# Moving two more tiles' inverse into the first down projection, and running the row halves of gate and up in two staggered passes

## The chip, the cores and the metric

The kernel runs on one core of one Trainium2 chip. The metric is the device time of one execution in microseconds (us), taken as the median of several executions. The span of the profile is about 2.0 us shorter than the time of the same execution.

## The reference, cut to what matters

```python
S, D, F = 2048, 576, 4608
h  = x + irfft2(rfft2(layernorm(x)) * (w_r + 1j * w_i))     # spectral mixing
n  = layernorm(h)
h2 = h + (gelu(n @ w_gate) * (n @ w_up)) @ w_down           # gated feed-forward
```

Everything is bf16 with f32 accumulation. The 2048 rows are 16 tiles of 128. The feed-forward takes them in four blocks of four tiles (512 columns of the moving operand).

## The kernel before: the parts that matter

TensorE makes the matmuls and leaves their sums in banks of PSUM; VectorE, ScalarE and POOL do the element-wise work. A helper records the operations of every engine in program order and derives the semaphore waits from named tiles (`r=` reads, `w=` writes). So each engine is handed its own list in this order, and a wait stands wherever an operand or a PSUM bank is not ready.

**Inverse transform.** For tile `c`, `st_I` makes 6 matmuls and a copy to SBUF; `st_N` makes 4 more, and VectorE adds the result to `x`. Ten tiles are done up front (`NPRE = 10`), the other six later.

**Way into the feed-forward.** The first four tiles are normalised by VectorE or POOL and transposed on TensorE (`turn_pe`, 5 small matmuls), and ScalarE copies the transpose to SBUF as `HT0`.

```python
TURN = (8, 9, 9, 9)                    # after which inverse tile each transpose stands
for c in range(1, NPRE):
    if c >= 2: st_I(c)
    st_N(c - 1)
    ...                                # squares, statistics
    if c == 6: ln2_b(0); ln2_c(0); norm(0, DVE); norm(1, POOL)
    if c == 7: norm(2, DVE); norm(3, POOL)
    for i in range(4):
        if TURN[i] == c: turn_pe(i)
```

**Gate and up.** D = 576 is 4.5 times 128, so the contraction is cut in slices of 64 rows: each output column needs 9 matmuls on the lower row half of the array and 9 on the upper half. In this kernel's trace a matmul of one half, which the program has write another bank, runs together with one of the other half: 648 of them take 70.05 us, a pair 0.216 us, while six without a partner take 1.45 us. Before, half 1 lags six positions behind half 0:

```python
ASEQ = [(0, i) for i in range(4)] + [(0, 8)] + [(1, 4 + i) for i in range(4)]   # half 0: gate, then up
BSEQ = [(0, i) for i in range(4)] + [(1, 4 + i) for i in range(4)] + [(1, 8)]   # half 1
LAG = 6
def gu(n):
    for s_ in range(9 * (n - 1) + LAG, 9 * n + LAG):
        for half in range(2):
            m, j = divmod(s_ - LAG * half, 9)
            ...
            b = 2 * (m % 3) + o                       # three pairs of PSUM banks
            P.op(PE, ... matmul(bank(b), ...[h0:h0 + 64, ...]))
    if n == 0:
        st_N(NPRE - 1)                                # last inverse tile, behind the first 6 matmuls
        return
    P.op(ACT, ... GL <- gelu(gate bank))
    P.op(DVE, ... AT[f] <- GL * up bank)              # the product
```

So the first six matmuls of half 0 have no partner: the last inverse tile, which needs the whole array, follows. In blocks 1 to 3 the columns are made in the order f = 9 ... 35, 0 ... 8.

**Down projection.** Each unit (half of a tile's columns) sums f = 0 ... 35. In block 0 each unit also carries the inverse of one deferred tile in a cheaper form (`def_i`, 8 small matmuls, then `def_n`, 2 matmuls).

```python
for h, (d0, d1) in enumerate(((0, cut), (cut, D))):
    b = (6, 7, 2, 3)[2 * (p % 2) * (tb > 0) + h]
    cd = NPRE + 2 * p + h if tb == 0 else NT
    if cd < NT: def_i(cd)
    for f in range(36):
        if cd < NT and f == 28: def_n(cd)
        P.op(PE, ... matmul(bank(b), AT[:, f, ...], WD[:, f, d0:d1], start=(f == 0), stop=(f == 35)))
    P.op(DVE, ... OS <- bank(b) + XO)                 # the output add
```

## Time and profile before

| what | value |
|---|---|
| time, median of 3 | 501.17 us (501.12 to 501.2) |
| the profiled execution | 502.36 us, span 500.6 us |
| TensorE busy | 490.3 us, 98% |
| a pair of half-row matmuls | 70.05 us / 324 = 0.216 us |
| a down matmul | 35.39 us / 288 = 0.123 us |

The page of the kernel before: busy time of TensorE, its granted clock in 40 slices of 12.5 us (9 is 90% or more), and the two costliest groups of matmuls.

```profile
PE 490.3 (98%) x4323; PEld 297.6 (59%) x4323; DVE 192.9 (39%) x418; ACT 159.3 (32%) x299; POOL 38.4 (8%) x51
...
PEclk9999989999999999999999999999999999999999
...
L920 PE MATMUL PS<-HT,WG 64*128 64x512 bf16 x2106 | 233.7, 378 | 0.9 <-ACT HT L862 0.9
...
L973 PE MATMUL PS<-WD,AT 128*128 128x288 bf16 (+2 forms) x1152 | 143.6, 286 | 0.0
```

The 378 ns of a group's mean are the time from start to end of one matmul, not its cost: the matmuls overlap in the trace, 324 pairs in 70.05 us. So the pace has to be read from the chain. The last columns say that TensorE waited 0.9 us in all before the gate/up matmuls and not at all before the down matmuls.

The chain of waits of the kernel before, in order of time: start, duration, what.

```profile
66.16 1.96 ACT HT L862 x3
...
68.26 1.45 PE PS L920 x6
69.71 0.86 PE PS L813 x4
70.57 71.42 PE PS L920 x648
...
172.10 9.80 PE PS L973 x80
181.90 70.05 PE PS L920 x648
251.94 35.39 PE PS L973 x288
287.33 70.05 PE PS L920 x648
```

The dense stream starts at 70.57 us. Block 0 takes 71.42 us where the others take 70.05: its first part ran at half clock. I call such a stretch of half clock a cut. The same profile by microsecond (TensorE busy, then granted clock, DMA share, GB/s):

```profile
69.00:70.00 1.00, 1.00 (x7) 0.95 1.00 300
70.00:71.00 1.00, 1.00 (x7) 0.50 1.07 373
71.00:72.00 1.00, 1.00 (x8) 0.50 1.01 378
72.00:73.00 1.00, 1.00 (x6) 0.50 1.05 396
73.00:74.00 1.00, 1.00 (x10) 0.84 0.97 369
```

The end of gate/up and the start of down in block 1 (timeline: start, duration, engine):

```profile
250.96 0.60 ACT L932 ACTIVATE GL<-PS 128x512 bf16<-128x512 f32 x1 [1.35 <-PE PS L920]
...
251.88 4.34 PE L973 MATMUL PS<-WD,AT 128*128 128x288 bf16 x34
252.05 0.69 DVE L933 TENSOR_TENSOR AT<-GL,PS 128x512 bf16<-128x512 bf16 x1 [1.26 <-PE PS L920]
```

The GELU of the last column is over at 251.56 us, before down starts. Its product ends at 252.74 us. The ninth step of down, which needs it, is due at 251.94 + 8 x 0.123 = 252.92 us. So it just fits, by 0.18 us.

### The profile page before, as it was taken

The page shows a single profiled execution, that of the slowest core. Times are in us where ns is not written, and L with a number is a line of the kernel's source. Part 1 is how long each engine was busy: PE and PEld are TensorE (multiplying, and loading weights), DVE is VectorE, ACT ScalarE, POOL GpSimd, SP SyncE. Part 2 cuts the span into 40 slices and gives each one's busy share as a digit, 9 for nine tenths or more (in the row PEclk, how much of TensorE's full clock was granted, in tenths as well). Part 3 has the DMA queues.
Part 4 walks back from the last instruction along what each step waited for, and adds up shares of the span by engine and source line. Part 5 has one row for each costly group of instructions (what it writes and reads, how often), then busy time and mean ns, then how long its engine had stood idle before and what let it go on. Part 6 is the DMA issues. An engine that isn't in the chain of part 4 may idle for free.

```text
span 500.6 us, 10028 instructions
## 1 busy us (share of the span) xinstructions
PE 490.3 (98%) x4323; PEld 297.6 (59%) x4323; DVE 192.9 (39%) x418; ACT 159.3 (32%) x299; POOL 38.4 (8%) x51
## 2 busy tenths in 40 slices
PE   6899989999999999999999999999999999999998
PEld 2688744444468864444477744444677544444775
DVE  6899643344355424433311134433200233333111
ACT  7888755342321322323300033232100123233000
POOL 3553270100000000000000000000000000000000
PEclk9999989999999999999999999999999999999999
DMA  8765796601000061100000001100000000000000
GB/s 277 171 199 197 254 356 243 214 14 25 18 7 14 19 211 32 22 14 1 2 13 12 19 18 22 22 1 1 1 18 19 13 1 2 1 2 1 12 19 19
DMA packets 27164, 31.40 MB, mean 63 GB/s; under 512 B 11664, under 2 KB 20112, under 8 KB 27120
## 3 DMA queue, kind: packets, MB, share of 16 engines
q1 hardware_dynamic: 24224, 18.81, 13.1%
q0 software_dynamic: 2896, 11.95, 6.7%
q8 instruction: 34, 0.56, 0.5%
q14 instruction: 10, 0.08, 0.1%
HBM read 26.42 MB, written 2.36 MB: 57 GB/s over the span
## 4 chain that ended last, share of the span: by engine, by line
PE 90%; DVE 6%; issue 1%; ACT 1%; DMA 1%; DVEq 0%
PE PS L920 57%; PE PS L973 28%; DVE TP L667 2%; PE PS L774 2%; DVE ST L468 1%; PE PS L813 1%; DVE ZS L672 1%; PE PS L628 1%; PE PS L940 1%; DVE CUS L641 1%; PE PS L691 1%; DMA XO<-in_A_x_dram 1%; DVE U L533 0%; ACT HT L862 0%; PE PS L657 0%
## 5 line engine op out<-in xcount | busy, mean ns | idle before, releaser
L920 PE MATMUL PS<-HT,WG 64*128 64x512 bf16 x2106 | 233.7, 378 | 0.9 <-ACT HT L862 0.9
L920 PEld LDWEIGHTS PS<-HT,WG 64*128 64x128 bf16 x2106 | 113.1, 94 | 117.7 <-issue 3.8
L932 ACT ACTIVATE GL<-PS 128x512 bf16<-128x512 f32 x144 | 85.8, 597 | 256.9 <-PE PS L920 256.1
L933 DVE TENSOR_TENSOR AT<-GL,PS 128x512 bf16<-128x512 bf16 x144 | 99.0, 688 | 174.5 <-PE PS L920 171.0
L973 PE MATMUL PS<-WD,AT 128*128 128x288 bf16 (+2 forms) x1152 | 143.6, 286 | 0.0
L973 PEld LDWEIGHTS PS<-WD,AT 128*128 128x128 bf16 x1152 | 110.8, 98 | 30.9 <-issue 1.3
L920 PE MATMUL PS<-HT,WGX 64*128 64x512 bf16 x486 | 56.9, 376 | 0.0
L976 DVE TENSOR_TENSOR OS<-PS,XO 128x288 bf16<-128x288 f32 (+2 forms) x32 | 14.7, 458 | 103.6 <-PE PS L973 103.6
L920 PEld LDWEIGHTS PS<-HT,WGX 64*128 64x128 bf16 x486 | 27.0, 94 | 27.3 <-PE PS L920 0.3
L712 POOL TENSOR_SCALAR WS<-WS 128x290 bf16<-128x290 bf16 x16 | 16.4, 1027 | 9.1 <-DMA WS<-in_A_w_i_dram 8.0
L628 PE MATMUL PS<-FT,U 128*128 128x290 bf16 x96 | 14.4, 287 | 0.5 <-DVE U L533 0.5
L691 PE MATMUL PS<-VT,ZS 128*128 128x256 bf16 x102 | 13.5, 272 | 0.2 <-DVE ZS L672 0.2
L667 DVE TENSOR_TENSOR TP<-YS,WS 128x580 bf16<-128x580 bf16 (+2 forms) x32 | 13.4, 457 | 0.3 <-issue 0.3
L704 ACT ACTIVATE V<-PS 128x768 bf16<-128x768 f32 x15 | 12.0, 811 | 1.0 <-PE PS L691 0.9
L804 ACT ACTIVATE JD<-XO 128x576 bf16<-128x576 bf16 x6 | 4.1, 684 | 24.8 <-DVE XO L957 24.8
L660 ACT ACTIVATE YS<-PS 128x578 bf16<-128x578 f32 x16 | 10.5, 655 | 3.5 <-PE PS L657 2.7
L522 PE MATMUL PS<-ATS,XO 128*128 128x128 bf16 (+1 forms) x80 | 7.1, 223 | 4.1 <-POOL ATS L495 2.7
L657 PE MATMUL PS<-CUS,BT 128*128 128x289 bf16 (+2 forms) x96 | 10.7, 246 | 0.3 <-DVE CUS L641 0.3
L628 PEld LDWEIGHTS PS<-FT,U 128*128 128x128 bf16 x96 | 9.2, 98 | 3.0 <-issue 0.7
L691 PEld LDWEIGHTS PS<-VT,ZS 128*128 128x128 bf16 x102 | 9.3, 97 | 1.7 <-issue 0.6
L816 DVE SCALAR_TENSOR_TENSOR XO<-PS,XO 128x576 bf16<-128x576 f32 x10 | 7.5, 755 | 6.7 <-PE PS L813 6.7
L468 DVE BATCH_NORM_STATS2 ST<-XO 128x6 f32<-128x288 bf16 x22 | 8.4, 445 | 3.8 <-DMA XO<-in_A_x_dram 3.8
(74 smaller groups left out, 200.4 us busy)
## 6 DMA issues: line engine op xcount, KB each, us to landing
WD<-in_B_w_down_dram POOLq DMA_DIRECT2D x9, 576.0 KB, 10.3
WG<-in_B_w_up_dram SPq DMA_DIRECT2D x4, 1152.0 KB, 6.6
WG<-in_B_w_gate_dram POOLq DMA_DIRECT2D x4, 1152.0 KB, 9.9
out_dram<-OS SPq DMA_DIRECT2D x30, 72.0 KB, 1.6
XO<-in_A_x_dram SPq DMA_DIRECT2D x3, 576.0 KB, 7.8
WGX<-in_B_w_gate_dram POOLq DMA_DIRECT2D x1, 1152.0 KB, 6.0
WGX<-in_B_w_up_dram SPq DMA_DIRECT2D x1, 1152.0 KB, 5.9
HT<-HN SPq DMA_TRANSPOSE x60, 2.4
```

Source lines behind the costliest of these rows:

```text
L468: P.op(DVE, lambda v, c=c, h=h: v.bn_stats(ST1[:, c, h, :], XO[:, c, 288 * h:288 * h + 288]), r=[("X", c)], w=[("ST1", c, h)])
L628: P.op(PE, lambda t, b=b, o=o, dt=dt, us=us, g=g: t.matmul(bank(b, 0, 128, 0, 2 * HK), U[:, us, g, :, :], FT[:, o, dt, :], start=(dt == 0) ...
L657: P.op(PE, lambda t, b=b, tb=tb, pl=pl, q0=q0, q1=q1, m=m, s3=s3, sp_=sp_: t.matmul(bank(b, 0, 128, q0, q1), BT[:, sp_, tb, :], CUS[:, s3, ...
L667: P.op(DVE, lambda v: v.tensor_tensor(out, YS[:, sl, :, q0:q1], WS[:, g, w_, q0:q1], op=ALU.mult), r=[("Y", sl), ("Wn", i), "Yz", "Zz"] + ...
L691: P.op(PE, lambda t, b=b, o=o, zp=zp, lhs=lhs, sp_=sp_, m=m, n=len(parts): t.matmul(bank(b, 0, 128, o, o + 256), lhs, VT[:, sp_, zp, :], s ...
L704: P.op(ACT, lambda a, dst=dst, src=src: a.activation(dst, src, ACTF.Copy), r=[("PS", bs[0]), ("PS", bs[2])], w=[("V", g, c) for c in range ...
L712: P.op(POOL, lambda v, g=GORD[i]: v.tensor_scalar(WS[:, g, 0, :], WS[:, g, 2, :], -1.0, None, op0=ALU.mult), r=[k for k in wkeys[0 if 1 <= ...
L920: op = P.op(PE, lambda t, h0=h0, kt=kt, wt=wt, f=f, slot=slot, b=b, HT=HT, s=(half == 0 and j in (0, 5)), e=(half == 1 and j in (3, 8)): t ...
L932: P.op(ACT, lambda a, s2=s2, b0=b0: a.activation(GL[:, s2, :], bank(b0), ACTF.Gelu_apprx_tanh), r=[("PS", b0)], w=[("GL", s2)])
L933: P.op(DVE, lambda v, s2=s2, b0=b0, f=f: v.tensor_tensor(AT[:, f, :], GL[:, s2, :], bank(b0 + 1), op=ALU.mult), r=[("GL", s2), ("PS", b0 + ...
L973: P.op(PE, lambda t, b=b, d0=d0, d1=d1, f=f, p=p: t.matmul(bank(b, 0, 128, 0, d1 - d0), AT[:, f, 128 * p:128 * p + 128], WD[:, f, d0:d1], ...
L976: P.op(DVE, lambda v, b=b, d0=d0, d1=d1, p=p, c=c: v.tensor_tensor(OS[:, p % 2, d0:d1], bank(b, 0, 128, 0, d1 - d0), XO[:, c, d0:d1], op=A ...
```

## The change

The intent: eight tiles' inverse moves into the first down projection instead of six, and the inverse in front is reordered so that normalisation and transposes start earlier, in smaller batches (three tiles, then one). Gate and up get a new order: in a first pass half 0 works on gate and half 1 on up (5 matmuls each), in a second pass they swap (4 each), and the second pass of a column follows the first pass of the next. Each pair of matmuls is thus complete from the first one on. It takes four pairs of PSUM banks, so the down projection moves from banks 6 and 7 to 0 and 1.

```diff
-NPRE = 10
+NPRE = 8
...
-    QR = ((0, 4), (4, NPRE), (NPRE, NT))
+    QR = ((0, 3), (3, 4), (4, NPRE), (NPRE, NT))
...
+    st_N(4); sq(3); ln2_c(0)                  # (one call a line in the source)
+    norm(0, DVE); norm(1, POOL); norm(2, POOL)
+    ln2_a(1); st_I(6); ln2_b(1); st_N(5); st_I(7); ln2_c(1)
+    norm(3, DVE)
+    turn_pe(0, ACT); st_N(6); turn_pe(1, DVE); turn_pe(2, ACT); turn_pe(3, ACT)
+    st_N(7)
...
+    FIRST = ([(0, i) for i in range(4)] + [(0, 8)], [(1, 4 + i) for i in range(4)] + [(1, 8)])
+    SECOND = ([(1, 4 + i) for i in range(4)], [(0, i) for i in range(4)])
+    def gu_part(m, second):
+        seqs = SECOND if second else FIRST
+        for j in range(len(seqs[0])):
+            for half in range(2):
+                o, wt = seqs[half][j]
...
-                b = 2 * (m % 3) + o
+                b = 2 * (m % 4) + o
...
-            b = (6, 7, 2, 3)[2 * (p % 2) * (tb > 0) + h]
+            b = (0, 1, 2, 3)[2 * (p % 2) * (tb > 0) + h]
...
-                if cd < NT and f == 28:
+                if cd < NT and f == 22:
...
-            gu(36 * tb + f + 1)
+            gu_part(36 * tb + f, False)
+            if f:
+                gu_part(36 * tb + f - 1, True)
...
+        gu_part(36 * tb + 35, True)
```

More of the change, by code (lines that the diff above doesn't have):

```diff
@@ L760, in _build @@
     vkeys = vk[0] + vk[1] + vk[2]
-    TURN = (8, 9, 9, 9)
-    seq = [("I", 0), ("I", 1)]
-    for c in range(2, NPRE):
-        seq += [("I", c)] + [("T", i) for i in range(4) if TURN[i] == c]
-    seq = {k: i % 2 for i, k in enumerate(seq)}
+    ISEQ = [("I", c) for c in range(8)] + [("T", i) for i in range(4)]
+    seq = {k: i % 2 for i, k in enumerate(ISEQ)}
     def islot(c):
@@ L836, in ln2_c, with lq @@
         P.op(DVE, lambda v, c0=c0, c1=c1: v.reciprocal(RS2[:, c0:c1], RS2[:, c0:c1]), r=[("SD2", q)], w=[("RS2", q)])
+    def lq(c):
+        return sum(c >= q0 for q0, _ in QR) - 1
     def norm(c, eng=DVE):
         hs = c % 4
-        q = (c >= 4) + (c >= NPRE)
+        q = lq(c)
         for i, (o0, o1, x0, x1) in enumerate(((0, D, 0, D), (D, 640, 512, D))):
@@ L852, in turn_dma, with turn_pe @@
                   r=[("HN", hs, 0), ("HN", hs, 1)], w=[("HT", q % 2, c % 4, k)], transpose=True)
-    def turn_pe(c):
+    def turn_pe(c, eng):
         hs = c % 4
@@ L859, in turn_pe, with sq @@
             b, o = b0 + k // 4, 128 * (k % 4)
-            P.op(PE, lambda t, b=b, o=o, k=k, hs=hs: t.matmul(bank(b, 0, 128, o, o + 128), HN[:, hs, 128 * k:128 * k + 128], IDT[:, :], start=True, stop=True),
+            lhs = HN[:, hs, 128 * k:128 * k + 128]
+            P.op(PE, lambda t, b=b, o=o, lhs=lhs: t.matmul(bank(b, 0, 128, o, o + 128), lhs, IDT[:, :], start=True, stop=True),
                  r=[("HN", hs, 0), ("HN", hs, 1), "IDT"], w=[("PS", b)])
-        P.op(ACT, lambda a, t0=t0, t1=t1, b0=b0: a.activation(HT0[:, 0:5, t0:t1], PS[:, b0 * 512:b0 * 512 + 640].rearrange("p (k e) -> p k e", k=5), ACTF.Copy),
-             r=[("PS", b0), ("PS", b0 + 1)], w=[("HT", 0, c, 0)])
-    st_I01()
-    for c in range(1, NPRE):
-        if c >= 2:
-            st_I(c)
-        st_N(c - 1)
-        if 2 <= c < 6:
-            square(c - 2, OS[:, c % 2, :], ("OS", c % 2, 0))
-        if c == 5:
-            ln2_a(0)
-        if c == 6:
-            ln2_b(0)
-            ln2_c(0)
-            norm(0, DVE)
-            norm(1, POOL)
-        if c == 7:
-            norm(2, DVE)
-            norm(3, POOL)
-        for i in range(4):
-            if TURN[i] == c:
-                turn_pe(i)
+        dst, src = HT0[:, 0:5, t0:t1], PS[:, b0 * 512:b0 * 512 + 640].rearrange("p (k e) -> p k e", k=5)
+        fn = (lambda a: a.activation(dst, src, ACTF.Copy)) if eng == ACT else (lambda v: v.tensor_copy(dst, src))
+        P.op(eng, fn, r=[("PS", b0), ("PS", b0 + 1)], w=[("HT", 0, c, 0)])
+    def sq(c):
+        square(c, OS[:, c % 2, :], ("OS", c % 2, 0))
+    st_I01()
+    st_N(0)
+    st_I(2)
+    st_N(1)
+    sq(0)
+    st_I(3)
+    st_N(2)
+    sq(1)
+    st_I(4)
+    st_N(3)
+    sq(2)
+    ln2_a(0)
+    st_I(5)
+    ln2_b(0)
+    st_N(4)
+    sq(3)
+    ln2_c(0)
+    norm(0, DVE)
+    norm(1, POOL)
+    norm(2, POOL)
+    ln2_a(1)
+    st_I(6)
+    ln2_b(1)
+    st_N(5)
+    st_I(7)
+    ln2_c(1)
+    norm(3, DVE)
+    turn_pe(0, ACT)
+    st_N(6)
+    turn_pe(1, DVE)
+    turn_pe(2, ACT)
+    turn_pe(3, ACT)
+    st_N(7)
     P.alias(ukeys + [(n_, a) for n_ in ("CU", "SU") for a in range(3)], [("WD", j) for j in range(9)])
@@ L895, in _build @@
     fnew = ([("AT", f) for f in range(36)] + [("GL", 0), ("GL", 1)] + [("HT", 1, i, k) for i in range(4) for k in range(5)])
-    ASEQ = [(0, i) for i in range(4)] + [(0, 8)] + [(1, 4 + i) for i in range(4)]
-    BSEQ = [(0, i) for i in range(4)] + [(1, 4 + i) for i in range(4)] + [(1, 8)]
-    LAG = 6
-    half_done = {}
     def fidx(m):
         return m % 36 if m < 36 else (m % 36 + 9) % 36
-    def gu(n):
-        for s_ in range(9 * (n - 1) + LAG, 9 * n + LAG):
-            for half in range(2):
-                m, j = divmod(s_ - LAG * half, 9)
-                if not 0 <= m < 144:
-                    continue
-                tb, f = m // 36, fidx(m)
-                slot = f // 9 if m < 27 else (3, 1, 2, 0)[f // 9]
-                o, wt = (ASEQ, BSEQ)[half][j]
+    FIRST = ([(0, i) for i in range(4)] + [(0, 8)], [(1, 4 + i) for i in range(4)] + [(1, 8)])
+    SECOND = ([(1, 4 + i) for i in range(4)], [(0, i) for i in range(4)])
+    first_done = {}
+    def gu_part(m, second):
+        tb, f = m // 36, fidx(m)
+        slot = f // 9 if m < 27 else (3, 1, 2, 0)[f // 9]
+        HT = HTS[tb % 2]
+        seqs = SECOND if second else FIRST
+        n = len(seqs[0])
+        for j in range(n):
+            for half in range(2):
+                o, wt = seqs[half][j]
                 kt = 4 if wt == 8 else wt % 4
                 h0 = 64 * half
-                HT = HTS[tb % 2]
-                b = 2 * (m % 3) + o
-                aft = [half_done[m, o]] if half and (j == 0 or j == 4) else []
-                op = P.op(PE, lambda t, h0=h0, kt=kt, wt=wt, f=f, slot=slot, b=b, HT=HT, s=(half == 0 and j in (0, 5)), e=(half == 1 and j in (3, 8)): t.matmul(
+                b = 2 * (m % 4) + o
+                aft = [first_done[m, o]] if second and j == 0 else []
+                op = P.op(PE, lambda t, h0=h0, kt=kt, wt=wt, b=b, s=(not second and j == 0), e=(second and j == n - 1): t.matmul(
                     bank(b), wg_tile(slot)[h0:h0 + 64, wt, 128 * (f % 9):128 * (f % 9) + 128], HT[h0:h0 + 64, kt, :], start=s, stop=e),
@@ L923, in gu @@
                     w=[("PS", b)], after=aft)
-                if half == 0:
-                    half_done[m, o] = op
-        m = n - 1
-        if m < 0:
-            st_N(NPRE - 1)
-            P.alias(fdead, fnew)
+                if not second:
+                    first_done[m, o] = op
+        if not second:
             return
-        s2, b0, f = m % 2, 2 * (m % 3), fidx(m)
-        P.op(ACT, lambda a, s2=s2, b0=b0: a.activation(GL[:, s2, :], bank(b0), ACTF.Gelu_apprx_tanh), r=[("PS", b0)], w=[("GL", s2)])
-        P.op(DVE, lambda v, s2=s2, b0=b0, f=f: v.tensor_tensor(AT[:, f, :], GL[:, s2, :], bank(b0 + 1), op=ALU.mult),
+        s2, b0 = m % 2, 2 * (m % 4)
+        P.op(ACT, lambda a: a.activation(GL[:, s2, :], bank(b0), ACTF.Gelu_apprx_tanh), r=[("PS", b0)], w=[("GL", s2)])
+        P.op(DVE, lambda v: v.tensor_tensor(AT[:, f, :], GL[:, s2, :], bank(b0 + 1), op=ALU.mult),
              r=[("GL", s2), ("PS", b0 + 1)], w=[("AT", f)])
@@ L978, in down @@
             P.dma(SP, ov[:, c, d0:d1], OS[:, p % 2, d0:d1], f"so{p % 2}{h}", r=[("OS", p % 2, h)], w=[("OUT", p % 2, h)])
-    gu(0)
+    P.alias(fdead, fnew)
     for tb in range(4):
         for f in range(36):
-            gu(36 * tb + f + 1)
+            gu_part(36 * tb + f, False)
+            if f:
+                gu_part(36 * tb + f - 1, True)
             if tb == 0 and f == 10:
@@ L987, in _build @@
             if tb == 0 and f < NPRE - 4:
-                square(4 + f, OS[:, f % 2, :], ("OS", f % 2, 0))
-            if tb == 0 and f == 13:
-                ln2_a(1)
-                ln2_b(1)
-                ln2_c(1)
+                sq(4 + f)
+            if tb == 0 and f == 8:
+                ln2_a(2)
+                ln2_b(2)
+                ln2_c(2)
             f0, f1 = (15, 3) if tb == 0 else (2, 4)
@@ L999, in _build @@
         if tb == 0:
-            ln2_a(2)
-            ln2_b(2)
-            ln2_c(2)
+            ln2_a(3)
+            ln2_b(3)
+            ln2_c(3)
             P.alias(vkeys + ["DP", "ITD", "EB", "Q0", "Q1", "YB0", "YB1", "JD"], [("WG", 3, k) for k in range(4)])
```

## The prediction

> **What bounds the kernel now.** TensorE. The page has PE busy 490.3 of 500.6 us; the chain of waits gives it 90%, 57% in the gate/up matmuls and 28% in the down projection. In order of time, that chain gives gate/up of row blocks 1 to 3 70.05 us each (324 pairs of 64-row matmuls at 0.216 us) and down 35.39 us (288 matmuls at 0.123 us), without a gap. [...] Only the seams can change.
>
> **Seam 1, the inverse (53.1 to 70.6 us).** Each tile costs PE 0.75 + 0.49 us, so two tiles fewer remove 2.5 us. Six gate/up matmuls that run without a partner at 68.3 us (1.45 us; six others stand unpaired at the end of block 3, within its 70.05) go too. Against this, transposes now wait: POOL takes 1.5 us per normalised tile, so tile 2 is ready near 64.7 us; VectorE works off its list in order, so its copy of transpose 1 ends near 66.5 and holds transpose 3, which shares its banks. I estimate the full stream starts at 67.8 us, against 70.6: -2.8. Before, the granted clock fell to 0.5 from 70 to 73.2 us, and block 0 took 71.4 instead of 70.05. With more PE idle before it I expect about 1.7 us lost again in block 0: -2.4 in all at the end of gate/up 0.
>
> **Seam 2, first down.** Two more deferred tiles at 0.51 + 0.24 us: +1.5. The second part, now at step 22 (2.7 us after the first), should just be ready: at most 0.2 us of waiting, at the first unit.
>
> **Seam 3, first down to block 1.** Down moves from banks 6 and 7 to 0 and 1; the next block starts in 0 and 1. Its first up matmul must wait for the last output add (0.1 + 0.46 us): +0.6.
>
> **Seam 4, gate/up to down in blocks 1 to 3.** Before, the gate bank was complete five pairs (1.08 us) before the end, so the GELU was over and the last product ended 0.8 us into the down projection, whose ninth step (f = 8, 0.98 us in) needs it. Now gate and up end together, in a second pass that is last before down: 0.1 + 0.6 (GELU) + 0.03 + 0.69 (product) = 1.43 us plus a signal. PE waits about 0.5 us, three times: +1.5.
>
> **Sum:** 501.2 - 2.4 + 1.5 + 0.1 + 0.6 + 1.5 = 502.5. The start of gate/up and the slow clock are least certain; I shade this to 501.9 us, range 500.0 to 503.6 us. Chances: faster by over 2% 0.01, within 2% 0.98, slower by over 2% 0.01.
>
> **What would show it.** Right: gate/up starting near 67.8 us, transposes waiting for POOL and VectorE; clock low for some 3.4 us near the start of block 0; first down about 41.4 us; PE idle of about 0.6 us at the first gate/up of block 1, released by the output add; PE idle of about 0.5 us in the down projections of blocks 1 to 3, released by the product; unchanged 216 and 123 ns. Wrong: no idle at the seams, or another pace.
>
> **What would make it wrong.** If the clock is not cut in block 0, 1.7 us comes back and the result is near 500.3. If a second slow stretch comes, 504. If transposes wait less, up to 2 us less. If the row halves pair worse in the new order, every pair pays: 10 ns each would be 13 us.

That only the seams can change stands as the author's estimate from the two paces in the trace, 0.216 us a pair and 0.123 us a down matmul.

## The result, and the profile after

The changed kernel took 501.7 us (median of 4 runs, 501.46 to 502.11), the kernel before beside it 501.14 us (500.88 to 501.2). The ratio is 1.0013 with a 95% interval of 0.9996 to 1.003. A ratio is the mean time of one kernel's fast runs over that of the other's of the same rounds, so it is not quite the ratio of the medians.

The prediction of 501.9 us (500.0 to 503.6) holds. But the span of the profiled execution went the other way: 499.7 us, 0.9 us shorter than the 500.6 us of the profile before. That contradiction came first.

The page after, same lines as shown of before:

```profile
PE 487.6 (98%) x4322; PEld 290.5 (58%) x4323; DVE 197.3 (39%) x431; ACT 159.4 (32%) x299; POOL 37.4 (7%) x51
...
PEclk9899999999999999999999999999999999999999
...
L936 PE MATMUL PS<-HT,WG 64*128 64x512 bf16 x2106 | 229.1, 376 | 0.7 <-ACT HT L864 0.4
...
L986 PE MATMUL PS<-WD,AT 128*128 128x288 bf16 (+2 forms) x1152 | 144.8, 286 | 1.2 <-DVE AT L946 1.2
```

A new wait has appeared: 1.2 us before the down matmuls, released by the product. The slow slice has moved to 12.5 to 25 us, where TensorE is not the limit (in the kernel before it is busy for 10.7 of these 12.5 us, at full clock).

The chain of waits after:

```profile
65.08 0.75 DVE HT L864
65.87 0.47 PE PS L861 x5
66.36 0.71 ACT HT L864
67.21 70.11 PE PS L936 x648
137.32 0.61 PE PS L953 x8
...
178.84 0.47 DVE OS L989
179.36 70.11 PE PS L936 x647
249.56 0.61 ACT GL L945
250.19 0.70 DVE AT L946
250.93 34.47 PE PS L986 x280
285.41 70.05 PE PS L936 x648
```

Block 0 starts at 67.21 us and runs at full pace (70.11). The output add stands in the chain before block 1, and GELU and product stand in it before the ninth down matmul of block 1, where 280 of the 288 remain.

The way into block 0, TensorE alone (the last bracket is idle time and what ended it):

```profile
62.62 0.44 PE L861 MATMUL PS<-IDT,HN 128*128 128x128 bf16 x5 [0.16 <-DVE TM L822]
62.89 0.66 PE L810 MATMUL PS<-GS,IT 128*128 128x288 bf16 x4
63.91 0.45 PE L861 MATMUL PS<-IDT,HN 128*128 128x128 bf16 x5 [0.36 <-ACT GS L780]
64.66 0.44 PE L861 MATMUL PS<-IDT,HN 128*128 128x128 bf16 x5 [0.29 <-POOL HN L842]
65.87 0.45 PE L861 MATMUL PS<-IDT,HN 128*128 128x128 bf16 x5 [0.78 <-DVE HT L864]
66.16 0.66 PE L810 MATMUL PS<-GS,IT 128*128 128x288 bf16 x4
67.21 9.03 PE L936 MATMUL PS<-HT,WG 64*128 64x512 bf16 x82 [0.39 <-ACT HT L864]
```

All four transposes wait. The third waits for POOL's normalisation and the fourth for VectorE's copy of the second, whose banks it takes. Up to 62.4 us TensorE is busy without a break; from there it needs 4.8 us for about 2.1 us of work.

The way into block 1, one line of TensorE and one of VectorE:

```profile
178.84 0.46 DVE L989 TENSOR_TENSOR OS<-PS,XO 128x288 bf16<-128x288 f32 x1 [1.02 <-PE PS L986]
...
179.36 4.92 PE L936 MATMUL PS<-HT,WG 64*128 64x512 bf16 x44 [0.30 <-DVE OS L989]
```

### The profile page after: what moved, and what is told of

Read it like the earlier page. It is cut to its first block, busy times and chain, and to the rows that moved or that the text cites. A ratio compares the mean times of both kernels' runs of the same rounds, so it can differ in the third digit from the quotient of the medians.

```text
span 499.7 us, 9895 instructions
## 1 busy us (share of the span) xinstructions
PE 487.6 (98%) x4322; PEld 290.5 (58%) x4323; DVE 197.3 (39%) x431; ACT 159.4 (32%) x299; POOL 37.4 (7%) x51
## 4 chain that ended last, share of the span: by engine, by line
PE 88%; DVE 8%; issue 2%; ACT 1%; DMA 1%; DVEq 0%; ACTq 0%
PE PS L936 56%; PE PS L986 28%; DVE TP L667 2%; DVE ST L468 1%; PE PS L953 1%; PE PS L771 1%; DVE ZS L672 1%; DVE CUS L641 1%; PE PS L691 1%; DMA XO<-in_A_x_dram 1%; DVE XO L813 1%; PE PS L628 1%; DVE U L533 0%; DVE AT L946 0%; PE PS L810 0%
## 5 line engine op out<-in xcount | busy, mean ns | idle before, releaser
L936 PE MATMUL PS<-HT,WG 64*128 64x512 bf16 x2106 | 229.1, 376 | 0.7 <-ACT HT L864 0.4
L936 PEld LDWEIGHTS PS<-HT,WG 64*128 64x128 bf16 x2106 | 107.7, 94 | 120.4 <-issue 1.4
L936 PE MATMUL PS<-HT,WGX 64*128 64x512 bf16 x486 | 53.8, 376 | 0.0
L936 PEld LDWEIGHTS PS<-HT,WGX 64*128 64x128 bf16 x486 | 23.8, 94 | 28.8
L712 POOL TENSOR_SCALAR WS<-WS 128x290 bf16<-128x290 bf16 x16 | 15.4, 963 | 9.2 <-DMA WS<-in_A_w_i_dram 5.4
L801 ACT ACTIVATE JD<-XO 128x576 bf16<-128x576 bf16 x8 | 5.5, 683 | 28.5 <-DVE XO L970 28.5
L657 PE MATMUL PS<-CUS,BT 128*128 128x289 bf16 (+2 forms) x96 | 10.7, 246 | 0.3 <-DVE CUS L641 0.3
L657 PEld LDWEIGHTS PS<-CUS,BT 128*128 128x128 bf16 x96 | 8.3, 97 | 2.1 <-issue 0.5
```

The lines of the kernel that those rows point to most:

```text
L657: P.op(PE, lambda t, b=b, tb=tb, pl=pl, q0=q0, q1=q1, m=m, s3=s3, sp_=sp_: t.matmul(bank(b, 0, 128, q0, q1), BT[:, sp_, tb, :], CUS[:, s3, ...
L712: P.op(POOL, lambda v, g=GORD[i]: v.tensor_scalar(WS[:, g, 0, :], WS[:, g, 2, :], -1.0, None, op0=ALU.mult), r=[k for k in wkeys[0 if 1 <= ...
L936: op = P.op(PE, lambda t, h0=h0, kt=kt, wt=wt, b=b, s=(not second and j == 0), e=(second and j == n - 1): t.matmul(bank(b), wg_tile(slot)[ ...
```

## The experiments

Eleven runs were made, in three sets on three chips (e1 to e4, e5 to e8, e9 to e11). All gave correct results. The kernel before was run beside each set; the ratios are to its executions of the same set, of both groups. Only one execution of each run was profiled, so for the others "slow" or "not slow" is read from their times.

The theory: both streams run at a pace that the order of the work does not change, and the time is the sum of the seams (way into block 0, first down, into block 1, the three later downs), plus 1.4 to 1.8 us when the stretch of half clock falls into dense matmuls. The rivals: the new order is itself slower or faster in the stream; or something outside the span changed.

### e1: the kernel before, again

No edit. 

> The kernel before, unchanged, to see whether the stretch of half clock at 70 to 73.2 us of its profiled execution (which was timed at 502.36 us, 1.2 us over the median of the others) belongs to the kernel or to that one execution. Theory (it moves from execution to execution): the spans are near 499.4 us at a time of 501.1 us, about 1.2 us shorter than the profiled 500.6, and a new profile has block 0 of gate/up at about 70.1 us with the stretch somewhere else. Rival (it belongs to the kernel): every span is 500.6 us, block 0 takes 71.4 us again, and the changed kernel has more time outside its span.

Six executions: 501.0, 501.0, 501.6, 502.6, 502.9 and 503.0 us. The profiled one (501.63 us, span 499.4 us) has a full clock in every slice of its page and this line in its chain:

```profile
70.82 70.05 PE PS L920 x648
```

So the 71.42 us of the first profile belonged to that execution. The unchanged kernel has 43 timed executions, besides the first profiled one: 32 between 500.4 and 501.7 us (median 500.93) and 11 between 502.2 and 503.1 us (median 502.64). The recorded spans split in the same way (498.6 to 499.4 against 500.3 to 501.1 us). The profile I had read was one of the slower group, while the three times beside it were of the faster one. This answers the contradiction: compared like with like, the span of the changed kernel is longer, not shorter.

### e2: the new inverse and eight deferred tiles, with the old gate/up order and old banks

```diff
 # in the changed kernel
-            gu_part(36 * tb + f, False)
-            if f:
-                gu_part(36 * tb + f - 1, True)
+            gu(36 * tb + f + 1)                       # old function, last inverse tile inside gu(0)
-            b = (0, 1, 2, 3)[2 * (p % 2) * (tb > 0) + h]
+            b = (6, 7, 2, 3)[2 * (p % 2) * (tb > 0) + h]
```

> The changed kernel with the old gate/up order and old output banks: eight deferred tiles and the new inverse alone. Seam theory: gate/up starts at 67.2 us with six unpaired matmuls (1.3 us) and the last inverse tile (0.5 us) in front of the full stream, which so starts 1.8 us later than in the changed kernel; no wait of 0.6 us after the first down and none of 0.55 us in the three later ones. Span against the changed kernel: 1.8 - 0.6 - 1.65 = -0.45 us, so about 499.2 us without a slow stretch in a dense part, time about 501.2 us. Rival (the two-pass order or the fourth PSUM pair is itself a gain or a loss in the steady stream): the three later gate/up blocks take something else than the 70.05 to 70.11 us of both kernels.

Measured: 503.53 us (502.72 to 504.35), span of the profiled one 500.8 us, ratio 1.0044. The seams are as expected: no wait at any of the four places, later blocks 70.05 us, downs 35.39 us. What I had not expected is that all six executions were slow. The profile shows why (columns as above):

```profile
66.00:68.00 2.00, 1.11 (x8) 1.00 1.05 343
68.00:70.00 2.00, 2.00 (x13) 0.68 1.04 305
70.00:72.00 2.00, 2.00 (x12) 0.50 1.02 377
```

Block 0 took 71.51 us.

```profile
69.23 71.51 PE PS L937 x644
```

So with this half of the change alone all of six executions were slow, and without it the kernel would be at about 501.3 us as expected (e5 shows that). Three of the six lay about 1 us above the other three; why is open. It is hardly one more cut: the mean clock is 0.993 in all six, and 0.993 in the profiled one goes with two cuts (at 14.1 us and at 68.7 us), as 0.997 in the first profile goes with one.

### e3: the new gate/up order and the new banks, with ten tiles up front

The edit is the mirror image of e2's, made in the kernel before; the last inverse tile stands in front of the stream, as in the changed kernel. 

> The kernel before with the two-pass gate/up order and the new output banks, ten tiles' inverse up front in the old order: the other half of the change alone. Seam theory: the last inverse tile fits into the wait for the last transpose copy, full stream from about 68.3 us; first down 39.9 us as before, then a wait of 0.6 us; three later waits of 0.55 us. Against the changed kernel 1.1 us later at the start of the stream and 1.5 us less in the first down: -0.4 us, span about 499.3 us without a slow stretch, time about 501.3 us. Rival: the four waits were caused by the deferral, not by the stream, and do not appear here: span about 497.1 us.

Measured: 501.26 us (501.06 to 501.39), span 499.1 us, ratio 0.9997. All four new waits are there: the output add stands in the chain before block 1, the product before the ninth step of the three later downs. Its chain (the other two waits for the product look the same):

```profile
68.10 70.11 PE PS L918 x648
...
178.22 0.47 DVE OS L971
...
249.56 0.70 DVE AT L928
```

The rival, that the deferral made them, falls. The stream started at 68.10 us. And none of the six executions was slow.

e2 and e3 together split the change. With the new stream in both, eight tiles (median 501.66 us over ten executions) are 0.4 us worse than ten (501.26 us). Counted from the start of the inverse (53.16 us against 52.98), the stream starts 1.1 us earlier (after 14.05 us against 15.12) and the first down with its wait is 1.5 us longer (42.04 us against 40.53). The spans differ by 0.6 us because 0.2 us of that lies before the inverse.

### e4: the changed kernel without the two new waits

```diff
-            b = (0, 1, 2, 3)[2 * (p % 2) * (tb > 0) + h]
+            b = (6 if p == 3 else 0) + h if tb == 0 else (0, 1, 2, 3)[2 * (p % 2) + h]
-            for f in range(36):
+            for j in range(36):
+                f = j if tb == 0 else (j + 9) % 36    # in the order in which the products are made
-                ... start=(f == 0), stop=(f == 35)
+                ... start=(j == 0), stop=(j == 35)
```

> The changed kernel with the two new waits taken away by other banks and another order: the last unit of the first down writes banks 6 and 7, so that block 1 need not wait for its output add; the down projections of blocks 1 to 3 add the products in the order in which they are made, the last made last. Seam theory: 0.6 + 3 x 0.55 = 2.25 us less than the changed kernel, span about 497.4 us, time about 499.5 us, 0.3% below the kernel before. Rival (PE's waits there only stand in for another limit, for instance the output adds or the next block's start): the idle time reappears elsewhere and the span stays within 0.5 us of 499.6 us.

Measured: 499.12 us (498.69 to 499.55), span 497.5 us, ratio 0.9954. Its chain:

```profile
67.37 70.11 PE PS L936 x648
...
178.89 70.04 PE PS L936 x648
248.93 35.39 PE PS L987 x288
284.31 70.03 PE PS L936 x648
```

The waits are gone and nothing took their place. They were worth the expected 2.2 us of span.

### e5: e2 with its waits filled

Seven full-array matmuls on zeros, written to a bank that is free, stand where TensorE waited before the stream.

```diff
     turn_pe(2, ACT)
+    fill(4)               # matmul(bank(7), ZD[:, 0:128], ZD[:, :])
     turn_pe(3, ACT)
+    fill(3)
```

> The old gate/up stream behind the new inverse again, whose six timed executions all lay between 502.7 and 504.4 us and whose profile shows half clock from 68.6 to 72 us; now with seven full-array matmuls on zeros put into the two waits of TensorE before the stream (four ahead of the last transpose, three after it), where they should cost nothing. Idle theory (the clock is cut because TensorE stood idle for about 2.4 us between 62 and 67 us): no cut in block 0, block 0 at 70.1 us, all or nearly all times near 501.3 us. Rival (the six unpaired matmuls, which use half of the rows for 1.45 us, bring the cut, whatever stands before them): times stay near 503 us.

Measured: 501.13 us (500.95 to 501.29), block 0 70.05 us, none of six slow, against six of six in e2.

```profile
69.03 70.05 PE PS L943 x648
```

Useless work made the kernel shorter, from a ratio of 1.0044 (e2) to 0.9996. The six unpaired matmuls are still in it, so they alone do not bring the cut.

### e6: an attempt to bring back unpaired matmuls

```diff
-        for j in range(n):
-            for half in range(2):
+        # first pass of the first column only: all of half 0, then all of half 1
+        for j, half in [(j, half) for half in range(2) for j in range(n)]:
```

> The changed kernel with only the first pass of the first column in another order: five matmuls of one row half, then five of the other, so that ten run without a partner (2.16 us in place of 1.08). Unpaired theory: half clock in block 0 in most executions: 501.7 + 1.1 + 1.4 = about 504.2 us. Idle theory: the idle time before is as in the changed kernel, which shows no cut in four executions, so only the 1.1 us are paid: about 502.8 us.

Measured: 501.88 us (501.41 to 502.31), none slow. Neither expectation was met: block 0 grew by 0.2 us (70.32 against 70.11), not by 1.1.

```profile
66.89 70.32 PE PS L936 x648
```

The start times in the trace show what happened: the first matmul starts alone at 66.89 us, and from the second slot on two start together (at 67.11, 67.33, 67.54 and 67.75 us), though five of one half stand ahead of the other half's in the program. How this comes about is not shown: the trace does not name the half of a matmul. So the ten matmuls did not run one at a time, and this run says nothing about unpaired matmuls. In e2 and in the kernel before the six do (1.45 us for six); why is not shown either.

### e7: e4 with the last transpose in other banks

```diff
-        b0 = 2 * seq["T", c]
+        b0 = 6 if c == 3 else 2 * seq["T", c]
         # and the last inverse tile in banks 2 and 3 in place of 6 and 7
```

> The version with both new waits taken away, and in addition the last transpose written to banks 6 and 7 in place of those of the second transpose, so that it no longer waits for VectorE's copy (the last inverse tile takes banks 2 and 3 instead). Seam theory: the last transpose starts at about 64.95 us in place of 65.87, its copy follows the one before it on ScalarE, and the gate/up stream starts 0.6 us earlier: span about 496.9 us, time about 498.5 us. Rival (the start is set by POOL's normalisation or by the order of ScalarE alone): no change from 499.1 us.

Measured: 498.6 us (498.37 to 499.12), span 496.5 us, ratio 0.9946. The fourth transpose follows the third at once, and the stream starts at 66.34 us, 3.97 us after the first transpose; in the changed kernel it was 67.21 - 62.62 = 4.59 us. That is the expected 0.6 us; in time it is 0.5 us against e4, which ran on another chip. The fourth transpose's wait for a bank was a real limit of the new inverse.

### e8: e3 without the two new waits

The edits of e4 in the kernel of e3. 

> Ten tiles' inverse up front as before, the new gate/up order, and both new waits taken away. If the deferral of two tiles loses (1.5 us in the first down against 0.9 us at the start of the stream) this is 0.6 us better than the same with eight tiles: span about 496.9 us, time about 498.8 us. If the deferral gains, it is slower than 499.1 us.

Measured: 498.76 us (498.64 to 499.15), span 496.6 us, ratio 0.995. Against e4 this is 0.4 us of median time and 0.9 us of profiled span, of which 0.5 us is the later start of the inverse in e4 (53.32 us against 52.85). The two ran on different chips, so the size is soft; it agrees with the 0.4 us of e3 against the changed kernel.

### e9: e2 with a partner for each unpaired matmul

```diff
+                    if s_ < LAG:     # the same rows of the other half, into spare bank 5, thrown away
+                        P.op(PE, ... matmul(bank(5), wg_tile(0)[64:128, ...], HT[64:128, ...], start=True, stop=True))
```

> The old gate/up stream behind the new inverse again (six of six executions between 502.7 and 504.4 us), the waits of TensorE left as they are, but each of the six unpaired matmuls given a partner in the other row half that writes a spare bank and is thrown away. The pair should take the time of the one. The run before this one, meant to test the same with another order of the first pass, did not[...]. Unpaired theory: no cut in block 0, times near 501.3 us. Idle theory: the cut stays in most executions, times near 503 us. As filling the idle time alone removed it too, both may be needed; then this one shows no cut either.

Measured: 502.68 us; four of six executions slow (502.64 to 502.78), two not (500.97 and 501.63). So executions were slow with a partner for every matmul too. Whether the partners make it rarer (four of six against six of six) is too few executions to say. The profiled one was cut from 66.6 to 70.0 us, and the stream began at 66.97 us: no half-row matmul, paired or not, had run before this cut.

### e10: ten tiles up front, all of the repairs

e8, with the last transpose in banks 6 and 7, the last inverse tile in banks 2 and 3, and VectorE copying the third transpose. 

> Ten tiles' inverse up front, new gate/up order, both new waits taken away, and the last transpose in banks 6 and 7, the last inverse tile in banks 2 and 3, the copy of transpose 2 on VectorE. The transposes no longer queue behind one bank and one engine: the stream should start at about 67.4 us in place of 68.0: time about 498.2 us, the lowest of all. If VectorE's copy comes too late behind its two sums, no change from 498.76 us.

Measured: 498.48 us (498.33 to 498.67), span 496.4 us, ratio 0.9946 (0.9934 to 0.9959). By these medians it is 0.5% faster than the kernel before, 0.6% faster than the changed one, and the lowest median of all, though only by 0.1 us against e7, which is within the spread. The stream started 3.81 us after the first transpose, against 4.24 us in e8: 0.4 of the expected 0.6 us.

### e11: the changed kernel, again

No edit. 

> The changed kernel, unchanged, for more executions of it beside those of the kernel before. If the new order really takes the slow stretch out of the dense part, all six times lie between 501.3 and 502.2 us, while about one in three of the kernel before lies near 502.6 us and the others near 500.9 us. If it only had luck in four executions, some of these lie near 503.2 us.

Measured: 501.65 us (501.23 to 502.09), none of six slow; beside it, one of eleven executions of the kernel before was. In all, none of the ten executions of the changed kernel and none of the 36 of e3, e4, e6, e7, e8 and e10 was slow. Against the 32 faster executions of the kernel before (500.93 us), the changed kernel's ten (median 501.66 us) are 0.7 us, or 0.15%, slower.

## Why the prediction was right, and where it was not

**The sum of the seams.** The clean comparison is the trace of e1 (no slow stretch in dense work) with the trace after. In e1 the input arrived later and the inverse began at 53.65 us in place of 53.16, so its start is shifted by that.

| term | predicted | measured |
|---|---|---|
| start of the full stream | -2.8 us | 67.21 - (70.82 - 0.49) = -3.1 us |
| block 0 | +0.4 (1.7 of cut in place of 1.4) | 70.11 - 70.05 = +0.1 |
| first down and the wait into block 1 | +1.5 + 0.1 + 0.6 = +2.2 | 42.04 - 39.90 = +2.1 |
| waits in the three later downs | +1.5 | 318.04 - 316.32 = +1.7 |
| sum | +1.3 | +0.8 |

The measured sum is that of the times: 0.7 us.

**Pace.** Right. Apart from the cut blocks and e6's first, all blocks take 70.03 to 70.11 us and all downs without a wait 35.38 to 35.40 us, in every version. That is 0.216 us per pair of half-row matmuls of 512 columns; e5's full-array fills of 512 columns have the same pace (four take 0.86 us in its chain). That neither stream could be faster was the author's estimate; no run here shows a limit. So the two-pass order and the fourth bank pair gain nothing inside the stream.

**Seam 1, start of the stream.** Mechanism right: transposes wait for POOL (0.29 us; POOL takes 3.05 us for the normalisation of two tiles of 128 x 576 elements, VectorE 1.08 and 0.64 us for one) and for VectorE's copy (0.78 us), and e7 shows that the latter was worth 0.5 us. The start was predicted 0.6 us late (67.8 against 67.21): VectorE's copy of the second transpose ended at 65.83 us, not at 66.5. It did stand behind other work in the list: the transpose ends at 64.36 us, and the copy starts at 65.00, when the add of an inverse tile that stands before it (from 64.32 us, 0.75 us) is all but done. Of the 2.5 us that two tiles of inverse cost TensorE, only 1.1 us came through (e3 against the changed kernel), because transposes and normalisation had become the limit. The tiles cost 1.5 us again in the first down. So the deferral itself loses 0.4 us.

**Seam 1, the clock.** This is the step that was wrong: "With more PE idle before it I expect about 1.7 us lost again in block 0". The 1.7 us was an estimate, half of the 3.4 us at a clock of 0.50 in the profile before; that the idle time brings them was not shown. It measured 0: block 0 took 70.11 us in both profiles, and none of ten executions was slow. Also wrong was the base that went with it: I took the cut in the profile for a fixture of the kernel, while the 501.2 us to which I added the terms came from executions without it. The two errors, -1.2 us in the base and +1.7 us in block 0, nearly cancelled. The sum was still 502.5 us; the step from there to 501.9 us was a shading for which I named no mechanism. So it is luck that the number came within 0.2 us. My own check shows it: without a cut I had foretold 500.3 us, there was none, and it was 501.7 us. The range was also wide enough to hold 501.2 us, no change at all.

What decides the cut? That is not shown. The clock records of the two profiles, before and after, each hold one cut, of 3.413 us at a granted clock of 0.50 (69.90 to 73.31 us before, 14.34 to 17.75 us after). The table sets the suspects beside the slow executions: the six unpaired matmuls at the head of the stream, the time from 60 us to the first gate/up matmul in which TensorE was not busy, and the last wait in it, right before that matmul (profiled executions).

| version | unpaired | not busy, us | last wait, us | slow |
|---|---|---|---|---|
| before (also e1) | six | 1.26 | 0.89 | 11 of 43 |
| e2 | six | 2.48 | 0.89 | 6 of 6 |
| e9 | none | 2.48 | 0.89 | 4 of 6 |
| e5 | six | 1.06 | 0.24 | 0 of 6 |
| after (also e11) | none | 1.99 | 0.39 | 0 of 10 |
| e4 | none | 1.98 | 0.39 | 0 of 6 |
| e6 | one slot | 1.98 | 0.39 | 0 of 6 |
| e7 | none | 1.36 | none | 0 of 6 |
| e3, e8 | none | 0.76 | 0.39 | 0 of 12 |
| e10 | none | 0.33 | 0.24 | 0 of 6 |

Unpaired matmuls are neither needed (e9) nor enough (e5), and the sum of the waits does not sort the versions: 1.26 us with slow executions, 1.99 us without. The last wait does, 0.89 us against 0.39 us or less, but that is a pattern and not a cause: no run changed this wait alone. Nor does any column tell which execution is cut: the first profile of the kernel before was and e1 was not, with the same 1.26 and 0.89 us. What the runs show is that filling the waits took the slow executions from six of six to none of six (e2, e5), and that with the last inverse tile in front of the stream none of 46 executions was slow (the changed kernel, e3, e4, e6, e7, e8, e10).

**Seams 2 to 4.** Right, mechanism and size. First down: two tiles at 0.51 + 0.24 us, no wait before the second part. Into block 1: released by the output add, 0.6 us. Later downs: released by the product, 0.55 us each. e4 removed both waits and got the 2.2 us back, and e3 showed that they come from the new stream and banks.

Why so little moved: the new stream starts 2.1 us earlier by itself (15.1 us after the start of the inverse in e3, 17.2 us in e1), because six slots without a partner (1.3 us) are gone and the last inverse tile is hidden in a wait. In none of its 46 executions was it slow, while the kernel before loses 1.7 us (502.64 against 500.93) in 11 of 43. It gives about 2.3 us back in four new waits (e3 against e1), and the deferral costs 0.4 us more. Without the four waits (e4, e7, e10) the same ideas are worth 0.4 to 0.5%.

## What to carry to other kernels

When a dense stream keeps its pace in every order tried, as here (70.03 to 70.11 us a block), only its seams are left, and a reordering that pays at one seam must be checked at every other: which bank the next stage starts in, and which operand of the next stage is made last. Moving work off the busiest engine gains only as far as that engine was the limit at that place; here 2.5 us of matmuls removed gave 1.1 us. Before reading a profile, compare its own time with the other times of the same kernel: the profiled execution may be of the rarer kind, and a term read from it then belongs to the execution and not to the kernel.
